# Scans that read PSUM, and a router that shares the turning banks, in a fused linear attention and mixture-of-experts kernel

## The chip, the core and the metric

The kernel runs on one core of a Trainium2 chip, in one launch. A core has five engines with a queue of instructions each: TensorE (PE in the profile), VectorE (DVE), ScalarE (ACT), GpSimd (POOL) and SyncE (SP), which here only starts transfers. They meet through semaphores. Data lie in SBUF, the on-chip memory of 128 partitions, and in PSUM, eight banks into which TensorE writes its products. The metric is the device time of one launch in microseconds; it was 355.39 as the median of 3 runs, between 354.56 and 355.56.

## The reference

Two layers follow each other. The first is a gated linear attention over 4 batches, 8 heads, 768 tokens and a head width of 48; its result is turned into 3072 tokens of 384 values. The second is a mixture of 8 experts that sends every token to the one expert with the largest logit.

```python
# attention, per batch and head
state = alpha[t][:, None] * state + outer(k[t], v[t])   # 48 x 48, alpha in 0.8 .. 1.0
y[t] = q[t] @ state
...
# mixture of experts; x is (3072, 384)
logits = x @ w_gate + modality_bias[modality_id]
e_idx = np.argmax(logits, axis=1)
probs = softmax(logits); gate_w = probs[token, e_idx]
out[mask_e] = gate_w * (np.maximum(x[mask_e] @ w1[e], 0.0) @ w2[e])   # 384 -> 1024 -> 384
```

## The kernel before

**The loop.** The attention runs in NU = 24 steps, one per chunk of 128 tokens of one batch, for all 8 heads. Heads go in pairs: 112 partitions hold two heads' channels (48 and 48, with a gap), and KW = 512 columns hold four pairs of 128 tokens. A step's turned rows (`tn`, 1600 floats on each of 112 partitions, 700 KB) hold keys, queries and the gates alpha. VectorE makes two scans over the gates. The first runs backwards (`decay`, L277): a running product of alpha, set to a top value at each chunk's last token by a constant tile DR, with max; its result GF lies in a PSUM bank, and the keys times GF are `kh`. The second runs forwards (`decay_back`, L287): it starts from the reciprocals of GF at the chunk's first token, which a tile DF holds (zero elsewhere), with add, and overwrites GF; the queries times that are `qh`. `amin` (L281) is the chunk's whole decay. TensorE then makes `scores` (L312) from qh and kh, `state` (L332), `outputs` (L339), `update` of the running 48 x 48 states (L357), and transposes: `natural` (L300) turns kh, `rows` (L370) turns the finished output. ScalarE copies PSUM results out, GpSimd masks the scores (L317) and keeps the states (L361, L363), and SyncE loads and stores.

**The router runs along.** Products for the logits (L382, L396), ranks of tokens among those of the same expert (L471 to L477), counts (L571) and places (L607) are spread over the steps as Python generators; `advance(spot)` moves each on by one piece at three spots of a step: after `rows`, after `decay_back`, and, for pieces tagged PEQ, between the scores and the outputs. Their small products lie in a PSUM bank of their own, "rt", from which VectorE reads them. Two banks "tr" turn in a ring for `natural`, `rows` and `update`. Tokens of two experts are placed early, from the tokens known by then: `route_early` counts them, `places` makes a table entry, and `gather` fetches their rows by an indirect transfer of GpSimd.

**After the loop** the first early expert runs in plain fp32 (`first_unit`, L149) while the router finishes. From then on weights and activations are split in a high and a low part of fp32r, made by ScalarE and VectorE (`split`, L876 and L878), and each product is three matmuls (L1051 to L1053 in the second layer, L1070 to L1072 in the first). `store` scales rows by gathered gates (L1085) and GpSimd scatters them. `gates_flow` makes the gates of a stretch of tokens: exponentials on ScalarE (L713), sum and reciprocal on VectorE (L714 to L716), a transpose on TensorE (L719), a copy (L721) and a store; its second use covers the last four of the first 24 groups of tokens, the four that the first use left out.

**The order** of instructions on TensorE, VectorE and ScalarE is the order in which the code issues them, in the loop and behind it; GpSimd's too in the loop. Nothing is rescheduled, so an instruction that waits holds up all behind it on its engine.

## Time and profile before

| | |
|---|---|
| median of 3 runs | 355.39 us (354.56 to 355.56) |
| profiled execution, its span | 355.34 us, 353.6 us |
| busy: PE, DVE, ACT, POOL | 337.0, 214.0, 178.8, 166.4 us |
| the loop of 24 steps | about 4 to 124 us of the span |
| transfers of turned rows | 22 of 700.0 KB, the first two chunks in parts |

The page's lists give, for a group of equal instructions, their line, engine, names and shapes, the count, the busy time and mean of one, then the idle time of the engine just before them and what ended it. A row of the list of waits gives engine, tile and line, what it waited for, and total, times, longest. A row of a timeline gives start and length in microseconds from the start of the span, and in brackets the idle time of the engine before it. A stretch is a row of windows: its busy times per engine with the number of instructions, then PEclk, the TensorE clock that was granted as a share of the full one, the share of the transfer engines that was busy, and GB/s.

### The profile page before, as it was taken

What the parts mean: (1) busy time and instruction counts of PE and PEld (TensorE: products, weight loads), DVE (VectorE), ACT (ScalarE), POOL (GpSimd) and SP (SyncE); (2) the same over time, 40 slices, a digit from 0 to 9 for tenths busy, and PEclk for the clock granted to TensorE, in tenths of its full rate; (3) what the DMA queues carried; (4) which work ended last, traced back from release to release, by engine and by line L of the source; (5) the groups of instructions that cost most, each with busy time, mean ns of one, the idle gap of its engine ahead of it and who ended that gap; (6) DMA issues with size and microseconds to landing.
All of it is one profiled execution on the core that took longest, in us unless ns stands there. A gap on an engine that the chain in (4) does not pass through costs nothing. (4 is left out here: it accounts for less than half of the span.)

```text
span 353.6 us, 8671 instructions
## 1 busy us (share of the span) xinstructions
PE 337.0 (95%) x3419; PEld 291.8 (83%) x3419; DVE 214.0 (61%) x406; ACT 178.8 (51%) x341; POOL 166.4 (47%) x210
## 2 busy tenths in 40 slices
PE   8996999999989999998999999999999999999992
PEld 3775888888768778998989988998899888888991
DVE  6899979999999658876465054605442545045400
ACT  3675587778775543474554153425432534255310
POOL 8799386658584630462673256025512661220021
PEclk9999899999998999999999999999999999999998
DMA  8999897979952957968465156316531653010011
GB/s 240 267 282 283 227 285 210 253 228 258 245 170 81 384 182 279 328 211 295 130 191 180 49 181 219 91 44 219 185 97 60 219 180 115 22 46 4 2 46 52
DMA packets 29590, 62.23 MB, mean 176 GB/s; under 512 B 3401, under 2 KB 17896, under 8 KB 29540
## 3 DMA queue, kind: packets, MB, share of 16 engines
q1 hardware_dynamic: 25396, 51.83, 49.0%
q0 software_dynamic: 4000, 9.68, 8.0%
q8 instruction: 29, 0.48, 0.6%
q14 instruction: 21, 0.17, 0.1%
q10 hardware_dynamic: 144, 0.08, 0.1%
HBM read 52.12 MB, written 9.50 MB: 174 GB/s over the span
## 5 line engine op out<-in xcount | busy, mean ns | idle before, releaser
L1017 POOL DMA_INDIRECT out_dram<-os,odx x23 | 24.7, 1073 | 101.5 <-ACT os L1085 93.7
L1051 PE MATMUL sc<-w2H,hH 128*128 128x384 f32 x192 | 65.1, 339 | 0.0
L1053 PE MATMUL sc<-w2H,hL 128*128 128x384 f32 x192 | 64.2, 334 | 0.0
L1052 PE MATMUL sc<-w2L,hH 128*128 128x384 f32 x192 | 64.2, 334 | 0.0
L878 DVE TENSOR_TENSOR w1L<-w1r,w1H 128x768 fp32r<-128x768 f32 x24 | 22.0, 956 | 65.4 <-ACT w1H L876 62.6
L317 POOL TENSOR_SCALAR_AFFINE_SELECT scT<-scT 128x512 f32<-128x512 f32 x48 | 41.7, 891 | 28.8 <-ACT scT L316 28.7
L1070 PE MATMUL tr<-xH,w1H 128*128 128x512 f32 (+1 forms) x144 | 53.8, 374 | 0.0
L1072 PE MATMUL tr<-xH,w1L 128*128 128x512 f32 (+1 forms) x144 | 53.5, 372 | 0.0
L1071 PE MATMUL tr<-xL,w1H 128*128 128x512 f32 (+1 forms) x144 | 53.5, 371 | 0.0
L870 DVE SCALAR_TENSOR_TENSOR hL<-tr,hH 128x512 fp32r<-128x512 f32 x47 | 32.3, 689 | 31.8 <-ACT hH L868 27.0
L868 ACT ACTIVATE hH<-tr 128x512 fp32r<-128x512 f32 x47 | 28.0, 598 | 44.3 <-PE tr L1072 28.1
L1085 ACT ACTIVATE os<-sc,gg 128x384 f32<-128x384 f32 x23 | 13.4, 582 | 66.8 <-PE sc L1053 40.8
L736 POOL DMA_INDIRECT gg<-gd,idx x25 | 26.9, 1078 | 27.9 <-DMA gd<-gs 20.8
L1051 PEld LDWEIGHTS sc<-w2H,hH 128*128 128x128 f32 x192 | 36.0, 188 | 1.1 <-issue 1.0
L1052 PEld LDWEIGHTS sc<-w2L,hH 128*128 128x128 f32 x192 | 36.1, 188 | 0.0
L1053 PEld LDWEIGHTS sc<-w2H,hL 128*128 128x128 f32 x192 | 36.0, 188 | 0.0
L277 DVE TENSOR_TENSOR_SCAN kv<-tn,DR 112x512 f32<-112x512 f32 x24 | 32.9, 1373 | 3.5 <-DMA tn<-in_turned_dram 2.9
L730 POOL DMA_INDIRECT xg<-xd,idx x25 | 26.5, 1058 | 12.2 <-issue 4.6
L316 ACT COPY scT<-sc 128x512 f32<-128x512 f32 x48 | 25.8, 589 | 11.9 <-PE sc L312 11.6
L1072 PEld LDWEIGHTS tr<-xH,w1L 128*128 128x128 f32 x144 | 27.1, 188 | 4.7
L1070 PEld LDWEIGHTS tr<-xH,w1H 128*128 128x128 f32 x144 | 27.1, 188 | 4.6
L1071 PEld LDWEIGHTS tr<-xL,w1H 128*128 128x128 f32 x144 | 27.1, 188 | 4.6
(247 smaller groups left out, 601.2 us busy)
## 6 DMA issues: line engine op xcount, KB each, us to landing
tn<-in_turned_dram SPq DMA_DIRECT2D x22, 700.0 KB
w1r<-in_moe_w_dram SPq DMA_DIRECT2D x16, 768.0 KB
w2r<-in_moe_w_dram SPq DMA_DIRECT2D x16, 768.0 KB
vt<-in_rowsv_dram SPq DMA_DIRECT2D x24, 192.0 KB
xd<-xs SPq DMA_DIRECT2D x24, 192.0 KB
tn<-in_turned_dram SPq DMA_DIRECT2D x4, 224.0 KB
tn<-in_turned_dram SPq DMA_DIRECT2D x2, 252.0 KB
xg<-xd,idx POOLq DMA_INDIRECT x25
```

The source lines that it names most:

```text
L277: vec.tensor_tensor_scan(GF[:, ::-1], alphas(i, 1, KW + 1)[:, ::-1], DR[:, ::-1], 0.0, op0=ALU.mult, op1=ALU.max)
L317: pool.affine_select(s, s, [[0, NP], [1, P]], ALU.is_ge, 0.0, base=0, channel_multiplier=-1)
L730: pool.indirect_dma_start(xg[x][:, u], None, xd[0:rows], IOA(idx[:, c : c + 1], 0), bounds_check=rows - 1, oob_is_err=False)
L736: pool.indirect_dma_start(gg[x][:, u : u + 1], None, gd[0:rows], IOA(idx[:, c : c + 1], 0), bounds_check=rows - 1, oob_is_err=False)
L868: act.activation(hH, hp, AF.Relu)
L870: vec.scalar_tensor_tensor(hL, hp, 0.0, hH.bitcast(F32), op0=ALU.max, op1=ALU.subtract)
L1051: pe.matmul(op, hH[:, us] if f is None else hH[:, f, us], wH, start=first, stop=False)
L1052: pe.matmul(op, hH[:, us] if f is None else hH[:, f, us], wL, start=False, stop=False)
L1053: pe.matmul(op, hL[:, us] if f is None else hL[:, f, us], wH, start=False, stop=final)
L1070: pe.matmul(hp, wH[:, d, fs], XH[:, d, :n], start=(d == 0), stop=False)
L1071: pe.matmul(hp, wH[:, d, fs], XL[:, d, :n], start=False, stop=False)
L1072: pe.matmul(hp, wL[:, d, fs], XH[:, d, :n], start=False, stop=(d == ND - 1))
```

## The change

**The scans.** DR moves to a PSUM bank (the one "rt" had); its top value is 2^-20 instead of 1. DF and the two GpSimd fills of it go. The reciprocals are taken inside GF, just before the second scan, and that scan runs in place, GF to GF, with max instead of add. `amin` is scaled back by 2^20 in one instruction. The turned rows carry 16 columns behind the second half instead of 64, 1552 floats in all.

One chunk's step on VectorE, before (DR and DF are the constant tiles, kv is the bank of GF, tn the turned rows):

```order
L277 SCALAR_TENSOR_TENSOR kv<-tn_83,DR 112x512
L280 RECIPROCAL DF_141<-kv 112x4
L281 TENSOR_TENSOR amin<-kv,tn_83 112x4
L283 TENSOR_TENSOR kh<-tn_83,kv 112x512
L287 SCALAR_TENSOR_TENSOR kv<-tn_83,DF_141 112x512
L289 TENSOR_TENSOR qh<-tn_83,kv 112x512
```

and now:

```order
L280 SCALAR_TENSOR_TENSOR kv<-tn_83,DR 112x512
L283 SCALAR_TENSOR_TENSOR amin<-kv,tn_83 112x4
L287 TENSOR_TENSOR kh<-tn_83,kv 112x512
L291 RECIPROCAL kv<-kv 112x4
L292 SCALAR_TENSOR_TENSOR kv<-tn_83,kv 112x512
L294 TENSOR_TENSOR qh<-tn_83,kv 112x512
```

The reciprocal has moved from behind the first scan to directly ahead of the second, and no instruction of the step reads two large inputs from SBUF.

**The router's products.** "rt" shares the two turning banks in the loop. A new helper `settle` has ScalarE copy such a product to an SBUF tile "kept", which VectorE reads; behind the loop it does nothing. There are nine such copies. A fourth spot END stands at the end of a step, behind `update`, and the early count takes it. On TensorE, at the step of the first early count, before (ohs are the counts so far, ones a constant):

```order
L332 MATMUL y<-qh,T_146 64x128 x8
L312 MATMUL sc<-qh,kh 64x128 x16
L571 LDWEIGHTS ones
L571 MATMUL rt<-ohs,ones 128x8
L339 MATMUL y<-scT,vt_88 64x128 x8
L357 MATMUL tr<-vt_89,knat 64x48
```

and now:

```order
L362 MATMUL tr<-vt_89,knat 64x48
L362 MATMUL tr<-vt_89,knat 48x48
L583 LDWEIGHTS ones
L583 MATMUL tr<-ohs,ones 128x8
L305 MATMUL tr<-ident,kh 128x112 x4
L375 MATMUL tr<-ident,yt 128x128 x4
```

The count has moved from between the scores and the outputs to behind the update's last product, and into a turning bank.

**Smaller moves.** Two GpSimd operations that make `hz` go ahead of the loop. `places` is split: the indices are made at once, ahead of the gather, and the positions of all early tokens once, later. At the start of the MoE the index operations stand ahead of the second split of the first-layer weights, and `gates_flow` starts one piece sooner: its exponentials right behind the four splits, its transpose L719 behind the first block of 18 first-layer products instead of the third, its store ahead of a weight load. One more store of tokens stands ahead of the first weights on SyncE. On VectorE there, before (w1L and w2L are low parts of weights, hL of activations, gt the gates):

```order
L670 TENSOR_TENSOR meta<-more,fli 1x1
L878 TENSOR_TENSOR w1L<-w1r_95,w1H 128x768 x2
L870 SCALAR_TENSOR_TENSOR hL<-tr,hH 128x512
L878 TENSOR_TENSOR w2L<-w2r_96,w2H 128x768
L714 TENSOR_REDUCE sm<-ls 128x4
L715 TENSOR_SCALAR sm<-sm 128x4
L716 RECIPROCAL gt<-sm 128x4
L870 SCALAR_TENSOR_TENSOR hL<-tr,hH 128x512
```

and now:

```order
L685 TENSOR_TENSOR meta<-more,fli 1x1
L894 TENSOR_TENSOR w1L<-w1r_95,w1H 128x768 x3
L729 TENSOR_REDUCE sm<-ls 128x4
L730 TENSOR_SCALAR sm<-sm 128x4
L731 RECIPROCAL gt<-sm 128x4
L886 SCALAR_TENSOR_TENSOR hL<-tr,hH 128x512
```

The three gate operations have moved from behind the first activations and a second-layer split to directly behind the first-layer splits.

The diff:

```diff
...
 NP = H // 2
 W = 64 + D
 KW = NP * P
-AW = KW + 64
+AW = KW + 16
 RW = 2 * KW + AW
 DM = H * D
 E = 8
...
 NJ = N // T
 MID = 2048
 EMPTY = 8192
-ALPHA_MAX_BITS = 0x3FA00000
+ALPHA_MAX_BITS = 0x3F800000
 AMIN = 1.0e-17
 AFLOOR = 1.0e-30
+TOP = 2.0**-20
 
 GROUPS = ((7, 0, 8), (15, 8, 16), (19, 16, 20), (23, 20, 24))
 LB = 4
...
     ps = ctx.enter_context(tc.tile_pool(name="ps", bufs=1, space=PSUM))
     loop_ps = ExitStack()
     lps = loop_ps.enter_context(tc.tile_pool(name="lps", bufs=1, space=PSUM))
-    ring = {"tr": (lps, "tr", 2), "rt": (lps, "rt", 1), "lg": (lps, "tr", 2)}
+    ring = {"tr": (lps, "tr", 2), "rt": (lps, "tr", 2), "lg": (lps, "tr", 2)}
 
     def ring_tile(r, shape):
         p, name, bufs = ring[r]
...
 
     def place(shape):
         return ring_tile("rt", shape)
+
+    def settle(t, shape):
+        if ring["rt"][0] is not lps:
+            return t
+        c = sb.tile(shape, F32, name="kept", bufs=2)
+        act.copy(c, t)
+        return c
 
     def turns(shape):
         return ring_tile("lg", shape)
...
-    mi = ac.tile([NU, P, 2], I32, name="mi")
-    DR = na.tile([W, KW], F32, name="DR")
+    mi = na.tile([NU, P, 2], I32, name="mi")
+    DR = lps.tile([P, KW], F32, name="DR")[:W]
     vec.memset(DR, AFLOOR)
-    vec.memset(DR[:, P - 1 :: P], 1.0)
-    DF = []
-    for i in range(2):
-        t = na.tile([W, KW], F32, name=f"DF{i}")
-        pool.memset(t, 0.0)
-        DF.append(t)
+    vec.memset(DR[:, P - 1 :: P], TOP)
     na.tile([P, 56], F32, name="padr")
     T1 = []
     for i in range(3):
...
         vec.tensor_tensor_scan(
             GF[:, ::-1], alphas(i, 1, KW + 1)[:, ::-1], DR[:, ::-1], 0.0, op0=ALU.mult, op1=ALU.max
         )
-        vec.reciprocal(DF[i % 2][:, ::P], GF[:, ::P])
-        vec.tensor_tensor(amin[:, i], GF[:, ::P], alphas(i, KW + 1, KW + 1 + NP), op=ALU.mult)
+        vec.scalar_tensor_tensor(
+            amin[:, i], GF[:, ::P], 1.0 / TOP, alphas(i, KW + 1, KW + 1 + NP), op0=ALU.mult, op1=ALU.mult
+        )
         kh = sb.tile([W, NP, P], F32, name="kh", bufs=3)
         vec.tensor_tensor(kh.rearrange("p a b -> p (a b)"), keys(i, 0), GF, op=ALU.mult)
         st[i, "k"] = kh
 
     def decay_back(i):
-        vec.tensor_tensor_scan(GF, alphas(i, 0, KW), DF[i % 2], 0.0, op0=ALU.mult, op1=ALU.add)
+        vec.reciprocal(GF[:, ::P], GF[:, ::P])
+        vec.tensor_tensor_scan(GF, alphas(i, 0, KW), GF, 0.0, op0=ALU.mult, op1=ALU.max)
         qh = sb.tile([W, NP, P], F32, name="qh", bufs=3)
         vec.tensor_tensor(qh.rearrange("p a b -> p (a b)"), keys(i, 1), GF, op=ALU.mult)
         st[i, "q"] = qh
...
         lp = turns([P, n, E]) if ring["lg"][0] is ps else place([P, n, E])
         for c in range(n):
             pe.matmul(lp[:, c], st[i, "l"][:, c], lsum, start=True, stop=True)
-        st[i, "lp"] = lp
+        st[i, "lp"] = settle(lp, [P, n, E])
 
     def logits_sum(i, n):
         z = slice(i + 1 - n, i + 1)
...
     odx = cp.tile([P, NH], I32, name="odx")
 
 
-    PEQ = "pe"
+    PEQ, END = "pe", "end"
 
     def route_begin():
         vec.memset(ohs, 0.0)
...
                 rp[:, t + 1 - t0 :], ones, oh[:, t].unsqueeze(1).broadcast_to([P, m, E]), start=False, stop=False
             )
         pe.matmul(rp, ones, ohs.unsqueeze(1).broadcast_to(sh), start=False, stop=True)
+        rp = settle(rp, [P, n, E])
         if side:
             yield
         vec.tensor_tensor(rk[:, s], rp, oh[:, s], op=ALU.mult)
...
     pos = cp.tile([P, NH], F32, name="pos")
     emp = cp.tile([P, NH], F32, name="emp")
 
+    hz = cp.tile([P, NS], F32, name="hz")
+    pool.tensor_scalar(hz, iof[:, 1 : NS + 1], float(U), None, op0=ALU.mult)
+    pool.tensor_scalar(hz, hz, zc, None, op0=ALU.is_le)
+
     def half_index():
-
-        hz = cp.tile([P, NS], F32, name="hz")
-        pool.tensor_scalar(hz, iof[:, 1 : NS + 1], float(U), None, op0=ALU.mult)
-        pool.tensor_scalar(hz, hz, zc, None, op0=ALU.is_le)
         vec.tensor_reduce(sz, hz, axis=AX.X, op=ALU.add)
 
-    def places(tp, z):
+    def places_in(tp, z):
+        vec.tensor_scalar(idx[:, z], tp, float(MID), 0.0, op0=ALU.add, op1=ALU.max)
+        vec.tensor_copy(vals[:, z], tp)
+
+    def places_out(z):
         v, p, e = vals[:, z], pos[:, z], emp[:, z]
-        vec.tensor_scalar(idx[:, z], tp, float(MID), 0.0, op0=ALU.add, op1=ALU.max)
-        vec.tensor_copy(v, tp)
         vec.tensor_scalar(p, v, 0.0, -1.0, op0=ALU.is_gt, op1=ALU.mult)
         vec.tensor_scalar(e, v, 0.0, float(EMPTY), op0=ALU.is_equal, op1=ALU.mult)
         vec.tensor_tensor(e, e, v, op=ALU.add)
-        return vec.scalar_tensor_tensor(odx[:, z], p, float(MID), e, op0=ALU.add, op1=ALU.add)
+        vec.scalar_tensor_tensor(odx[:, z], p, float(MID), e, op0=ALU.add, op1=ALU.add)
+
+    def places(tp, z):
+        places_in(tp, z)
+        places_out(z)
 
     def route_early(s, t0):
 
         n = EARLY[s]
-        yield PEQ
+        yield END
         cnt = place([P, E])
         pe.matmul(cnt, ones, ohs, start=True, stop=(s == 0))
         if s:
             pe.matmul(cnt, ones, left, start=False, stop=True)
+        cnt = settle(cnt, [P, E])
         yield
         if s:
             vec.scalar_tensor_tensor(first, cnt, float(TE), taken, op0=ALU.is_ge, op1=ALU.mult)
...
         tp = place([P, 2])
         for t in range(n):
             pe.matmul(tp, OL[:, t], OHE[:, t], start=(t == 0), stop=(t == n - 1))
-        yield
-        places(tp, slice(UE * s, UE * s + UE))
+        tp = settle(tp, [P, 2])
+        yield
+        places_in(tp, slice(UE * s, UE * s + UE))
         gather(s, early_cols(s), row(n))
         yield
         if s:
...
         vec.tensor_scalar(left, taken, -float(UE), None, op0=ALU.mult)
         if s == NA - 1:
             start_keys()
+            places_out(slice(0, UE * NA))
 
     def start_keys():
         for u in range(2):
...
     def advance(spot):
         for f in list(flows):
             tag, seen = flows[f]
-            if (tag == PEQ) != (spot == PEQ) or seen in ((now["s"], 2), (now["s"], PEQ)):
+            late = seen in ((now["s"], 2), (now["s"], PEQ), (now["s"], END))
+            if spot not in {PEQ: (PEQ,), END: (END,)}.get(tag, (1, 2)) or (late and spot != END):
                 continue
             go(f, spot)
 
...
             update(s - 1)
             if s == 1:
                 fill(2)
+        advance(END)
 
     mctx.close()
     mctx.enter_context(tc.manual_schedule(engines=manual))
...
         return None if keep else put(c, os)
 
     def layer2(h, w2, x, u, c, per, keep=False):
+        return store(layer2_sum(h, w2, u, per), x, u, c, keep)
+
+    def layer2_sum(h, w2, u, per):
         us = slice(u * P, (u + 1) * P)
         op = ps.tile([P, DM], F32, name="sc", bufs=2)
         for f in range(NF):
             j, z = divmod(f, per)
             hf = h[j] if per == 1 else (h[j][0][:, z], h[j][1][:, z])
             products(op, None, hf, piece(w2[f // 2], f % 2), us, f == 0, f == NF - 1)
-        return store(op, x, u, c, keep)
+        return op
 
     def short(x, w, c):
         xp = ps.tile([P, ND, P], F32, name="sc", bufs=2)
...
 
     prep(1, UE)
     w1s = [split1(1, 0)]
-    layer2(hs[0], w2s[0], 0, 0, 0, 2)
-    w1s += [split1(1, 1)]
+    op0 = layer2_sum(hs[0], w2s[0], 0, 2)
     for _ in ends:
         pass
     gather(2, slot_cols(1))
+    store(op0, 0, 0, 0)
+    w1s += [split1(1, 1)]
     layer2(hs[0], w2s[0], 0, 1, 1, 2)
     w1s += [split1(1, j) for j in (2, 3)]
     seq = [("E", 1)] + [("S", i) for i in range(1, SU - 1)] + [("H", SU)] + [("S", SU - 1)]
     cols = [early_cols(0)] + [early_cols(e) if k == "E" else slot_cols(e)[: 1 if k == "H" else U] for k, e in seq]
     seq = [("E", 0)] + seq
     last_gates = gates_flow(EARLY[-1], NU)
+    next(last_gates)
     weights(0, expert(seq[2][1]))
     for n in range(1, len(seq)):
         kind, e = seq[n]
```

## The prediction

> **What bounds the kernel now.** I read the page's busy shares first, then the waits of PE, then PE, VectorE and ScalarE in order of time at the two places where the change moves work.
>
> ```profile
> PE 337.0 (95%) x3419; PEld 291.8 (83%) x3419; DVE 214.0 (61%) x406; ACT 178.8 (51%) x341; POOL 166.4 (47%) x210
> PE sc L312 <- issue: 1.5, 1, 1.5
> PE rt L571 <- DVE ohs L490: 1.5, 1, 1.5
> PE y L332 <- issue: 1.5, 1, 1.5
> PE tr L370 <- ACT yt L347: 1.1, 5, 0.3
> PE kv L1024 <- DMA xg<-xd,idx: 0.8, 1, 0.8
> PE tr L370 <- DVE emp L562: 0.5, 1, 0.5
> PE kv L719 <- PE tr L1072: 0.3, 1, 0.3
> ```
>
> PE is busy for 337.0 of the 353.6 us of the span, and everything else is at 61% or less. So a VectorE saving is worth nothing by itself; only PE's pauses and its clock can be shortened, and a new pause is paid in full. The waits list nearly all pauses after the first 20 us: 1.5 us at L571 (the router's count), 0.5 at L370, 0.8 at L1024, 0.3 at L719, and two of 1.5 us whose cause is "issue".
>
> The pauses cost more than their length. These windows are 3.41 us long and hold, in this order, two around the pause at L332, which a window's boundary cuts, two around that at L312 and two around that at L571, and last a long one of the loop for comparison; the columns are span, busy us and instruction count per engine, then PEclk.
>
> ```profile
> 23.90:27.32 3.42, 3.06 (x53) 2.44 (x49) 3.26 (x3) 3.21 (x7) 3.36 (x4) 1.00 1.05 306
> 27.32:30.74 3.42, 2.33 (x59) 2.15 (x60) 3.25 (x6) 1.31 (x4) 3.18 (x5) 1.00 1.03 286
> 34.15:37.56 3.41, 1.89 (x30) 1.55 (x24) 2.97 (x8) 1.38 (x4) 1.45 (x3) 1.00 1.04 272
> 37.56:40.98 3.42, 3.42 (x30) 2.67 (x30) 3.32 (x7) 1.35 (x3) 1.64 (x2) 0.50 0.93 261
> 102.42:105.83 3.41, 1.94 (x56) 1.70 (x57) 3.31 (x9) 2.29 (x6) 3.10 (x4) 1.00 0.23 78
> 105.83:109.24 3.41, 3.41 (x37) 3.32 (x34) 3.31 (x6) 1.15 (x3) 1.68 (x2) 0.50 0.00 0
> 70.00:100.00 30.00, 29.57 (x593) 24.40 (x592) 28.83 (x48) 23.72 (x54) 20.17 (x23) 1.00 0.87 242
> ```
>
> A window with 1.5 us idle (3.41 - 1.89, 3.41 - 1.94) is followed by one at a granted clock of 0.50; a window with 1.1 idle (3.42 - 2.33) is not. A stretch at 0.50 does half of 3.41 us of work: about 1.7 us lost. So the pause at L571 costs 1.5 + 1.7 = 3.2 us. The Trainium skill (TensorE: Matmul & The Clock Gate, What's actually happening) says the same of the windows, 3413 ns at half rate or full, and adds that they are free-running; by that, which pause falls whole into one window changes between executions. No trace here shows a second execution.
>
> **Part 1, the scans.** One step of VectorE, with the wait at its end:
>
> ```profile
> 43.72 1.68 DVE L277 TENSOR_TENSOR_SCAN kv<-tn,DR 112x512 f32<-112x512 f32 x1
> 45.43 0.18 DVE L280 RECIPROCAL DF<-kv 112x4 f32<-112x4 f32 x1
> 45.53 0.13 DVE L281 TENSOR_TENSOR amin<-kv,tn 112x4 f32<-112x4 f32 x1
> 45.58 0.68 DVE L283 TENSOR_TENSOR kh<-tn,kv 112x512 f32<-112x512 f32 x1
> 46.29 1.23 DVE L287 TENSOR_TENSOR_SCAN kv<-tn,DF 112x512 f32<-112x512 f32 x1
> 47.56 0.69 DVE L289 TENSOR_TENSOR qh<-tn,kv 112x512 f32<-112x512 f32 x1
> 50.51 0.17 DVE L555 TENSOR_REDUCE sz<-hz 128x1 f32<-128x13 f32 x1 [2.26 <-POOL hz L554]
> 50.59 1.23 DVE L277 TENSOR_TENSOR_SCAN kv<-tn,DR 112x512 f32<-112x512 f32 x1
> L277 DVE TENSOR_TENSOR_SCAN kv<-tn,DR 112x512 f32<-112x512 f32 x24 | 32.9, 1373 | 3.5 <-DMA tn<-in_turned_dram 2.9
> L287 DVE TENSOR_TENSOR_SCAN kv<-tn,DF 112x512 f32<-112x512 f32 x24 | 30.1, 1255 | 0.6
> L283 DVE TENSOR_TENSOR kh<-tn,kv 112x512 f32<-112x512 f32 x24 | 16.2, 676 | 0.0
> L317 POOL TENSOR_SCALAR_AFFINE_SELECT scT<-scT 128x512 f32<-128x512 f32 x48 | 41.7, 891 | 28.8 <-ACT scT L316 28.7
> ```
>
> The same scan takes 1.23 or 1.68 us. The products L283, which already take their second input from PSUM, keep to 0.68 throughout. I take it that a scan with two SBUF inputs is held up by GpSimd's work and one with its second input in PSUM is not. Then 48 scans at 1.23 are 59.0 instead of 63.0 us: -4.0. Against it: the reciprocal now hides, since L281 starts 0.10 after it; in its new place the scan waits for its result, so it costs about 0.2 instead of 0.1, and 24 of these are +2.4. The two index operations of POOL go ahead of the loop: the wait of 2.26 at L555 goes. VectorE gains 4.0 - 2.4 + 2.3 = 3.9 us by the loop's end.
>
> The Trainium skill (SBUF — State Buffer, Who interferes with whom) states this rule: two SBUF inputs contend with a GpSimd read, one does not. The rows of L277 and L283 agree.
>
> PE takes almost none of that: from 70 to 100 us it is busy for 29.57 of 30.00, and no pause in the list but the named ones is over 0.3 us. It may start its full stretch earlier, since in the first steps it does follow VectorE. A step's excess of scans is 4.0 / 24 = 0.17 us against 0.10 for the reciprocal, so four or five steps give 0.3, and the turned rows, 3% smaller (1552 floats for 1600), land a little sooner where VectorE waits for them (2.9 us in all at L277). I take -0.4, between 0 and -0.8.
>
> No row shows a scan with its second input in PSUM, nor one in place there. Bounds: 1.23, and 1.73 (the slowest scan now is of that order). I take 1.23, as products with and without PSUM do not differ that way; the rival below has the other end. The max in place of add is the same pass.
>
> **Part 2, the shared banks and the count.** Nine small ScalarE copies come in; the nearest row is the state's copy, 0.32 for 112x192, so about 0.2 each, 2 us of an engine at 51%. The copies of the logits stand behind score copies for which PE's next group does not wait. The count is different, and it is the main term:
>
> ```profile
> 102.88 1.05 PE L312 MATMUL sc<-qh,kh 48*64 48x128 f32 x32
> 105.40 0.17 PE L571 MATMUL rt<-ohs,ones 128*128 128x8 bf16 x1 [1.47 <-DVE ohs L490]
> 105.50 1.70 PE L339 MATMUL y<-scT,vt 128*64 128x128 f32 x16
> 104.95 0.40 DVE L490 TENSOR_TENSOR ohs<-ohs,hsum 128x8 bf16<-128x8 bf16 x1
> 101.43 0.32 ACT L359 COPY S<-tr 112x192 f32<-112x192 f32 x1
> ```
>
> Now it stands ahead of the outputs and makes PE wait until 105.35. Moved behind the update, it comes after the outputs' products, of which the row shows 1.70 us at half clock, so some 0.9 at full, and the update's, about half as much: 103.9 + 1.4 = 105.3, and VectorE, ahead by then, has its input earlier than 105.35. The wait is gone: -1.5, and the half-clock stretch behind it: -1.7. New: the count takes a turning bank right after the update's, so the next transposes (L300) wait for the copy of S: 0.3 + 0.1 = +0.4. The wait of 0.5 at L370 for the last of the place operations shrinks, since those move to later: -0.3. VectorE's lead does not run out: it gains 3.9 and PE 3.5.
>
> Loop: -1.5 - 1.7 + 0.4 - 0.3 - 0.4 = **-3.5**.
>
> **Part 3, the start of the MoE.** The last early gates' transpose (L719) moves on PE from behind the third block of first-layer products to behind the first. Blocks are 18 matmuls, 2.16 us. What it needs comes in this order (before's times):
>
> ```profile
> 151.61 0.28 PE L1070 MATMUL tr<-xH,w1H 128*128 128x256 f32 x1
> 153.76 0.28 PE L1070 MATMUL tr<-xH,w1H 128*128 128x256 f32 x1
> 158.56 0.27 PE L719 MATMUL kv<-ident,gt 128*4 128x128 f32 x1 [0.32 <-PE tr L1072]
> 153.10 0.58 ACT L1085 ACTIVATE os<-sc,gg 128x384 f32<-128x384 f32 x1 [0.83 <-DMA gg<-gd,idx]
> 153.58 1.56 ACT L876 CAST w1H<-w1r 128x768 fp32r<-128x768 f32 x2
> 154.70 1.83 DVE L878 TENSOR_TENSOR w1L<-w1r,w1H 128x768 fp32r<-128x768 f32 x2
> 157.91 0.18 DVE L714 TENSOR_REDUCE sm<-ls 128x4 f32<-128x32 f32 x1
> 158.33 0.18 DVE L716 RECIPROCAL gt<-sm 128x4 f32<-128x4 f32 x1
> ```
>
> In the new order PE would issue it at 153.8. The exponentials stand on ScalarE behind both casts (end 155.1), and these behind a store that waits for the gathered gates until 153.1. VectorE takes the sum behind the two low parts; these can begin when the first cast is done, about 154.4, and end at 156.2; sum to reciprocal is 0.6 more: 156.8. So PE waits 3.0. If the gates' gather were no limit, the store could go at about 151.8, as its products end when the first-layer ones begin (151.61), and all of it 1.3 earlier: 1.7. I take 2.7, nearer the measured end. In exchange the old waits go: 0.3 at L719, and 0.8 at L1024, whose gathers have that much longer. A pause of 2.7 puts more than 1.5 into one window nearly wherever the boundary falls: +1.7 for a half-clock stretch. Behind it all work is as before. Start of MoE: 2.7 - 0.3 - 0.8 + 1.7 = **+3.3**.
>
> The other moves (index operations before a split, a store of tokens ahead of the first weights, one ahead of a weight load) are off this path: none of them issues anything that PE's two changed pauses wait for.
>
> **Sum.** 353.6 - 3.5 + 3.3 = 353.4 of span, and with the 1.7 outside it (355.34 - 353.6) 355.1; the median of the runs, 355.39, is 0.05 above the profiled one. Forecast **355.2 us**, no change that can be measured: a difference under 0.3% (1.07 us) counts as none, since the runs of before spread over 1.0 us. Its own range is 354.3 to 356.4.
>
> **Rivals.** (a) The gate transpose's wait is short or cut by a window's boundary and costs no clock, so the gain of the loop shows: 355.2 - 1.7 = 353.5. For it: the gather that sets it lands late behind weight loads and could land sooner. Against: 1.5 in one window was enough twice. Chance 0.20.
>
> (b) The stretch at 37.56 goes too. Its pause starts at 34.34, just inside the window from 34.15; begun 0.4 earlier it leaves 1.3 in that window, between the 1.1 that did nothing and the 1.5 that did. 353.5, or with (a) 351.8. Chance 0.17, and 0.07 for both.
>
> (c) Slower: the gate transpose waits the full 3.0 and the boundary halves it, so that both windows hold 1.5 idle. Then the clock stays at half through the tail of the second and the whole third: 1.9/2 + 1.7 = 2.6 instead of 1.7, and with 0.3 more of wait and no gain in the first steps (0.4) 356.8. It decides from a wait of about 2.9 on. Chance 0.14.
>
> (d) Slower by the scans: at 1.37 each (L277's mean now) they take 48 x 0.14 = 6.7 us more than I assume. VectorE's gain becomes a loss of 2.8; PE then waits for it in the later steps, the loop's gain of 3.5 is lost and some clock with it: 359. It decides from about 0.08 us per scan. Against: products reading PSUM are not slower. Chance 0.06.
>
> The rest, 0.36, is the forecast.
>
> **How the numbers follow.** Faster: (a), (b) and both, 0.44. Slower: (c), (d) and a little of the forecast's upper edge, 0.22. Same: 0.34. The range from 351.5 to 357.2 takes in both (a) with (b) and (c) and leaves out (d) and the far ends.
>
> **What would show it.** Right: no wait at the count's matmul; scans all near 1.23; a wait of PE of 2 to 3 us for the reciprocal of the gates ahead of the second block of first-layer products; a clock of 0.50 behind it, none near 100 us. Wrong: no pause at the gate transpose (then 352 to 353.5), or scans over 1.3.

## The result

The changed kernel took 359.62 us as the median of 17 executions (355.92 to 362.46); the kernel before, beside it, 354.06 us (352.36 to 356.68). The ratio is 1.0119, with a 95% interval from 1.0089 to 1.0149: it is slower, by about 1.2%. A second series of ten executions gave 357.47 beside 354.46, a ratio of 1.0070 (1.0036 to 1.0103): slower again, by less. A ratio leaves out the executions more than 1.5% above the fastest of their kernel, while a median takes all, so that a kernel can have a ratio near 1 and a median 2 us above. The profiled execution of the changed kernel took 357.0 us with a span of 355.2, so it is one of its better ones. That matters below: the mean granted clock of an execution ran from 0.966 to 0.989, with a mean of 0.977, where the kernel before has 0.990 over the 138 executions that stood beside the experiments.

The waits of PE in the changed kernel, longest first, answer to the list of before:

```profile
PE kv L734 <- DVE gt L731: 2.6, 1, 2.6
PE tr L620 <- DVE OHE L614: 2.3, 1, 2.3
PE sc L317 <- issue: 1.0, 1, 1.0
PE y L337 <- issue: 0.9, 1, 0.9
PE tr L583 <- DVE ohs L496: 0.7, 1, 0.7
PE tr L375 <- ACT S L364: 0.5, 1, 0.5
```

Two waits are new. One is the gates' transpose (L734, was L719), 2.6 us, where 2.7 had been forecast. The other is the early places' product (L620, was L607), 2.3 us; nothing of that was forecast. The wait at the count (L583) has halved and not gone. The two pauses for which nothing shown is to blame are shorter, 0.9 and 1.0 instead of 1.5, and the half-clock stretch that began at 37.56 before is gone. Each of the new waits leaves PE idle for over 2 us of one window of 3.41 us (3.41 - 1.10, 3.41 - 1.38), and a window at half clock follows (columns as before):

```profile
112.72:116.13 3.41, 1.10 (x34) 0.85 (x25) 3.24 (x11) 1.23 (x3) 1.22 (x2) 1.00 1.03 386
116.13:119.55 3.42, 2.94 (x34) 2.77 (x31) 2.38 (x8) 0.91 (x2) 0.72 (x1) 0.50 1.05 380
153.68:157.09 3.41, 1.38 (x12) 1.38 (x13) 3.34 (x7) 1.92 (x5) 2.52 (x3) 1.00 0.90 268
157.09:160.51 3.42, 3.42 (x18) 3.42 (x17) 0.98 (x3) 1.32 (x2) 1.91 (x2) 0.50 1.02 392
```

VectorE's groups of one step and GpSimd's masks, now, and the last product of the queries on VectorE, now (L294) and before (L289):

```profile
L292 DVE TENSOR_TENSOR_SCAN kv<-tn,kv 112x512 f32<-112x512 f32 x24 | 29.5, 1228 | 0.8
L280 DVE TENSOR_TENSOR_SCAN kv<-tn,DR 112x512 f32<-112x512 f32 x24 | 29.4, 1226 | 3.1 <-DMA tn<-in_turned_dram 2.4
L283 DVE SCALAR_TENSOR_TENSOR amin<-kv,tn 112x4 f32<-112x4 f32 x24 | 3.9, 161 | 0.8
L322 POOL TENSOR_SCALAR_AFFINE_SELECT scT<-scT 128x512 f32<-128x512 f32 x48 | 29.9, 646 | 52.4 <-ACT scT L321 52.2
...
117.22 0.69 DVE L294 TENSOR_TENSOR qh<-tn,kv 112x512 f32<-112x512 f32 x1
```

```profile
117.94 0.69 DVE L289 TENSOR_TENSOR qh<-tn,kv 112x512 f32<-112x512 f32 x1
```

Both scans are at 1.23 us, as forecast, and GpSimd's masks have fallen from 891 to 646 ns: the scans and GpSimd no longer hold each other up. But VectorE reaches its last product of the queries only 0.7 us sooner (117.94 - 117.22), not 3.9.

### The profile page after: what moved, and what is told of

Same layout as the page of the kernel before. It is cut to its first block, busy times and chain, and to the rows that moved or that the text cites. A ratio compares the mean times of both kernels' runs of the same rounds, so it can differ in the third digit from the quotient of the medians.

```text
span 355.2 us, 8689 instructions
## 1 busy us (share of the span) xinstructions
PE 336.4 (95%) x3419; PEld 291.5 (82%) x3419; DVE 214.5 (60%) x402; ACT 179.9 (51%) x350; POOL 135.8 (38%) x208
## 5 line engine op out<-in xcount | busy, mean ns | idle before, releaser
L1034 POOL DMA_INDIRECT out_dram<-os,odx x23 | 23.0, 1002 | 111.3 <-ACT os L1102 98.6
L1089 PE MATMUL tr<-xH,w1L 128*128 128x512 f32 (+1 forms) x144 | 54.3, 377 | 0.0
L322 POOL TENSOR_SCALAR_AFFINE_SELECT scT<-scT 128x512 f32<-128x512 f32 x48 | 29.9, 646 | 52.4 <-ACT scT L321 52.2
L1089 PEld LDWEIGHTS tr<-xH,w1L 128*128 128x128 f32 x144 | 27.9, 194 | 4.7
L1087 PEld LDWEIGHTS tr<-xH,w1H 128*128 128x128 f32 x144 | 27.9, 194 | 4.6
L280 DVE TENSOR_TENSOR_SCAN kv<-tn,DR 112x512 f32<-112x512 f32 x24 | 29.4, 1226 | 3.1 <-DMA tn<-in_turned_dram 2.4
```

The source lines that it names most:

```text
L280: vec.tensor_tensor_scan(GF[:, ::-1], alphas(i, 1, KW + 1)[:, ::-1], DR[:, ::-1], 0.0, op0=ALU.mult, op1=ALU.max)
L322: pool.affine_select(s, s, [[0, NP], [1, P]], ALU.is_ge, 0.0, base=0, channel_multiplier=-1)
L1087: pe.matmul(hp, wH[:, d, fs], XH[:, d, :n], start=(d == 0), stop=False)
L1089: pe.matmul(hp, wL[:, d, fs], XH[:, d, :n], start=False, stop=(d == ND - 1))
```

## The experiments

Sixteen kernels were run, one of them the changed kernel again. Times are medians; "beside" is the kernel before, run beside it; the ratio has its 95% interval. The clock is the mean over the executions, without single ones of over 370 us.

| run | time | beside | ratio | clock |
|---|---|---|---|---|
| changed kernel | 359.62 | 354.06 | 1.0119 (1.0089 to 1.0149) | 0.977 |
| gates back | 359.8 | 354.94 | 1.0100 (1.0044 to 1.0157) | 0.982 |
| count back | 357.86 | 354.94 | 1.0055 (1.0017 to 1.0093) | 0.983 |
| both back | 357.54 | 354.94 | 1.0007 (0.9963 to 1.0050) | 0.987 |
| places at the end | 361.3 | 354.94 | 1.0135 (1.0071 to 1.0199) | 0.978 |
| loop only | 355.9 | 354.51 | 1.0030 (0.9990 to 1.0070) | 0.987 |
| MoE start only | 357.21 | 354.51 | 1.0079 (1.0050 to 1.0109) | 0.984 |
| count only | 355.25 | 354.51 | 1.0027 (0.9995 to 1.0059) | 0.987 |
| second scan only | 354.85 | 354.51 | 1.0012 (0.9981 to 1.0043) | 0.991 |
| index operations only | 353.34 | 354.46 | 0.9972 (0.9942 to 1.0002) | 0.993 |
| index operations and count | 354.68 | 354.46 | 1.0000 (0.9971 to 1.0029) | 0.992 |
| changed kernel again | 357.47 | 354.46 | 1.0070 (1.0036 to 1.0103) | 0.980 |
| idle matmuls, too long | 356.82 | 354.46 | 1.0086 (1.0056 to 1.0116) | 0.993 |
| idle matmuls, sized | 356.27 | 354.83 | 1.0022 (0.9988 to 1.0056) | 0.991 |
| index operations and smaller rows | 355.38 | 354.83 | 1.0009 (0.9975 to 1.0043) | 0.988 |
| index operations, again | 353.19 | 354.15 | 0.9980 (0.9945 to 1.0015) | 0.992 |
| the same with idle matmuls | 353.68 | 354.15 | 0.9976 (0.9938 to 1.0015) | 0.994 |

Medians of 6 or 12 executions are not exact to a microsecond: "both back" lies 2.6 us above its neighbour by the medians and has a ratio of 1.0007. Where two medians differ and the intervals of the ratios overlap, the difference is not shown.

### Undoing parts of the change

**Gates back.** The gates' flow starts one piece later again.

```diff
     last_gates = gates_flow(EARLY[-1], NU)
-    next(last_gates)
```

> The changed kernel, with only the last early gates started where they were before: exponentials behind the first block of first-layer products, transpose on PE behind the third. Theory A (the time comes from two new waits of PE, 2.6 us for the gates' reciprocal and 2.3 us for the places' one-hots, and the half clock behind each, 1.7 us): the wait of 2.6 and its half-clock stretch go, old waits of about 0.3 and 0.8 us return, so 3 us less than the changed kernel's 359.6: 356.5. Theory B (the loop itself is slower, by copies and small VectorE work): within 1 us of 359.6.

359.8 in six executions, no gain that can be seen. The wait of 2.6 us at the transpose is gone (0.4 is left), and another has come in its place; the first rows of the list of waits:

```profile
PE tr L620 <- DVE OHE L614: 2.3, 1, 2.3
PE sc L317 <- issue: 2.1, 1, 2.1
PE kv L1041 <- DMA xg<-xd,idx: 1.7, 2, 1.5
```

PE now waits 1.7 us for the gathered tokens of the next expert, and a stretch at half clock follows, from 169.11. In the changed kernel the wait at the transpose had covered this. That is why theory A's number was missed, as far as one profile can say it.

**Count back.** The early count stands between scores and outputs again.

```diff
         n = EARLY[s]
-        yield END
+        yield PEQ
```

> The changed kernel, with only the early count back between the scores and the outputs. Theory A: PE waits about 1.5 us at the count again, and the wait of 2.3 us for the places' one-hots shrinks by as much, since PE comes to them later: one wait of the two remains with a half-clock stretch, so 359.6 within 1 us. The prediction's own theory (the count's place is worth 3.2 us): 362.8.

357.86, 1.8 below the first series of the changed kernel and 0.4 above the second; the ratios overlap. The wait at the count is 2.2 us, and the one for the places is not in the list any more. So the count's new place did not save 3.2 us, which would have made this run 362.8. Whether it cost anything is not shown by this run.

**Both back.**

> The changed kernel, with both the gates and the count back in their old places; left are the scans in PSUM, the shared banks with their copies, the smaller rows and the earlier index work. Theory A: as with the gates alone, 356.5 within 1 us, so 2 above the kernel before. If scans and copies by themselves gain (the prediction): under 354.

357.54, 1 us over what theory A had, at a ratio that shows no loss. Its profiled execution came to the first early expert 2.1 us sooner than the kernel before (at 123.76 instead of 125.88) and lost that at the gathers:

```profile
PE kv L1041 <- DMA xg<-xd,idx: 4.4, 2, 2.2
```

**Places at the end.** The gates back, and the places' products behind the update as well.

```diff
-        yield PEQ
+        yield END
         tp = place([P, 2])
```

> The changed kernel with the gates back and, new, the early places' products also at the end of a step, behind the update, where the count stands. Theory A: the wait for the one-hots falls from 2.3 to about 0.8 us and its half-clock stretch goes, beside what the gates give: 359.6 - 3 - 1.5 - 1.7 = 353.4, about the kernel before. Theory B: 358 or more.

361.3, the slowest. The wait for the one-hots fell from 2.3 to 1.3 us, as far as the new place gave, and the next PE instruction that needs VectorE waited 1.8 instead. Here are the waits for VectorE in the order of the program, count, places, ranks:

```profile
PE tr L583 <- DVE ohs L496: 0.7, 1, 0.7
PE tr L620 <- DVE OHE L614: 1.3, 1, 1.3
PE sc L476 <- DVE oh L473: 1.8, 1, 1.8
```

Their sum is 3.8 us, against 0.7 + 2.3 = 3.0 in the changed kernel. So PE's wait does not hang on the place of one product: near the loop's end VectorE is behind, and moving a product that needs it changes where PE waits.

### Parts by themselves

**Loop only.** The changed kernel with count, gates and the start of the MoE as before; left are the scans, the shared banks and copies, the smaller rows and the earlier index work. The part of the edit at the start of the MoE (the other two are shown above):

```diff
-    op0 = layer2_sum(hs[0], w2s[0], 0, 2)
+    layer2(hs[0], w2s[0], 0, 0, 0, 2)
+    w1s += [split1(1, 1)]
     for _ in ends:
         pass
     gather(2, slot_cols(1))
-    store(op0, 0, 0, 0)
-    w1s += [split1(1, 1)]
```

> The changed kernel with the count back, the gates back and the start of the MoE in its old order (store and second split ahead of the index operations); left are the scans in PSUM, the shared banks with their copies, the smaller rows and the index work ahead of the loop. Theory C (with the count and the gates back, the time is lost at the start of the MoE, where the next expert's weights now start about 1.3 us sooner and crowd the gathers that PE waits for): like the kernel before, 354 to 355, some 2.5 us under the run with both back. Theory D (scans, copies or the VectorE work of the router cost it): 357 or more, as that run.

355.9, 1.4 above the kernel beside it, which its interval does not tell from nothing. By the medians it is 1.6 under the run with both back, as theory C has it, but the ratios, 1.0030 and 1.0007, show no such difference; only the profiles speak for theory C. The wait for the gathers is 0.5 us here and 4.4 there. The two issues of the next expert's first weights, among which the gathers are issued, take 2.44 us from the first start to the second end in the run with both back and 3.65 here:

```profile
152.50 2.44 SPq L717 DMA_DIRECT2D w1r<-in_moe_w_dram  x2
```

```profile
153.39 3.65 SPq L717 DMA_DIRECT2D w1r<-in_moe_w_dram  x2
```

So with the index operations ahead of the second split, the second load starts sooner, and the gathers land later: PE's last wait for them ends at 164.35 there and at 162.31 here. This rests on one profile of each; that the crowding is the cause was not tested by itself. Among the profiles with the old order this wait varies too, from 0.4 to 1.8 us, so only 4.4 and the 4.1 of the run with the places at the end stand clear of it.

**MoE start only.** The kernel before with the new order there, gates included (the reverse of the two edits above).

> The kernel before, with only the new order at the start of the MoE: index operations and gather ahead of store and second split, gates started one piece sooner. By the prediction's third part: 2.7 - 0.3 - 0.8 of waits and 1.7 of half clock, 354.9 + 3.3 = 358.2. Theory C and D alike expect a loss here, C 2 to 3 us; if the gates' wait only takes the place of a wait for the gathers, within 1 us of before.

357.21, 2.7 above the kernel beside it, clear of noise; the forecast's third part had 3.3. PE waits where it was forecast:

```profile
PE kv L719 <- DVE gt L716: 2.9, 1, 2.9
```

**Count only.** The kernel before with the spot END and the count there (the two main lines of the edit).

```diff
-        yield PEQ
+        yield END
...
+        advance(END)
```

> The kernel before, with only the early count moved to the end of a step, behind the update. By the prediction: the wait of 1.5 us and its half-clock stretch go, 354.9 - 3.2 = 351.7. Theory A (the wait moves on to the places' one-hots, since VectorE and not the place sets the time): 354.9 within 1 us, with PE waiting 1 to 2 us at the places' products. Slower than 356: the count's place delays the chain of count, places and gathers.

355.25, 0.7 above the kernel beside it, and within its interval of no change; theory A. The wait of 1.5 us has come apart, again into waits for VectorE and ScalarE, and the gathers are waited for longer (1.8 us instead of 0.8):

```profile
PE kv L1026 <- DMA xg<-xd,idx: 1.8, 2, 1.7
PE tr L300 <- DVE kh L283: 1.4, 1, 1.4
PE tr L370 <- DVE vals L560: 1.1, 1, 1.1
PE rt L396 <- ACT scT L316: 0.7, 1, 0.7
PE rt L571 <- DVE ohs L490: 0.6, 1, 0.6
```

**Second scan only.** Reciprocals inside GF, in place, with max; DR stays in SBUF.

```diff
-        vec.reciprocal(DF[i % 2][:, ::P], GF[:, ::P])
-        vec.tensor_tensor(amin[:, i], GF[:, ::P], alphas(i, KW + 1, KW + 1 + NP), op=ALU.mult)
+        vec.scalar_tensor_tensor(
+            amin[:, i], GF[:, ::P], 1.0 / TOP, alphas(i, KW + 1, KW + 1 + NP), op0=ALU.mult, op1=ALU.mult
+        )
...
-        vec.tensor_tensor_scan(GF, alphas(i, 0, KW), DF[i % 2], 0.0, op0=ALU.mult, op1=ALU.add)
+        vec.reciprocal(GF[:, ::P], GF[:, ::P])
+        vec.tensor_tensor_scan(GF, alphas(i, 0, KW), GF, 0.0, op0=ALU.mult, op1=ALU.max)
```

> The kernel before, with only the second scan changed: reciprocals inside GF just ahead of it, in place with max, no DF; the first scan keeps DR in SBUF. Second scans near 1.23 us instead of 1.255 (0.6 us in all), reciprocals no longer hidden (+2.4) and amin in the two-step form (+1.6): VectorE 3 us later at the loop's end. Theory D: since PE waits for VectorE at the count and later, 1 to 3 us slower than before, 356 to 358. If PE's lag behind VectorE covers it: 354.9 within 1 us.

354.85, no change that can be told. It shows the scans best, for one form stands beside the other: second inputs in SBUF for the first scan, in PSUM for the second. GpSimd's masks fall to 657 ns with it alone, so most of their gain comes from the second scan.

```profile
L273 DVE TENSOR_TENSOR_SCAN kv<-tn,DR 112x512 f32<-112x512 f32 x24 | 31.0, 1292 | 4.0 <-DMA tn<-in_turned_dram 3.4
L285 DVE TENSOR_TENSOR_SCAN kv<-tn,kv 112x512 f32<-112x512 f32 x24 | 29.5, 1228 | 0.8
```

**Index operations only.** Two small operations of GpSimd leave the loop.

```diff
+    hz = cp.tile([P, NS], F32, name="hz")
+    pool.tensor_scalar(hz, iof[:, 1 : NS + 1], float(U), None, op0=ALU.mult)
+    pool.tensor_scalar(hz, hz, zc, None, op0=ALU.is_le)
+
     def half_index():
-
-        hz = cp.tile([P, NS], F32, name="hz")
-        pool.tensor_scalar(hz, iof[:, 1 : NS + 1], float(U), None, op0=ALU.mult)
-        pool.tensor_scalar(hz, hz, zc, None, op0=ALU.is_le)
         vec.tensor_reduce(sz, hz, axis=AX.X, op=ALU.add)
```

> The kernel before, with only the two index operations of GpSimd moved ahead of the loop, so that VectorE no longer waits 2.3 us for them at step 9. If VectorE's lead decides at the count (theory A): its input comes 2.3 us sooner than 105.35, the wait of 1.5 us at the count and its half-clock stretch go: 354.6 - 3.2 = 351.4. If PE or the clock takes it back elsewhere: 354.6 within 1 us.

353.34, 1.1 under the kernel beside it. The same again:

> The kernel before with the two index operations ahead of the loop, once more. If the gain is real: 353.3 to 353.9, about 1 us under the kernel before, mean clock about 0.993. If it was chance: within 0.5 us of before.

353.19, 1.0 under. Each interval just takes in no change; the two agree, and the clock is up from 0.990 to 0.992 or 0.993. The forecast of 3.2 was too much: PE still waits 1.5 us at the count (2.1 in the second run), since it came there as much sooner as VectorE did: 101.58 instead of 103.93, and VectorE's input at 103.00 instead of 105.35.

**Index operations and count.** Both of the last edits on the kernel before.

> The kernel before, with the two index operations ahead of the loop and the count at the end of the step. Theory A: VectorE's 2.3 us are there for the places too, so neither the count nor the places make PE wait: 351.4, as with the index operations alone. If the count's place is bad in itself (a bank that waits for the copy of the states, later gathers): 0.5 to 1 us more than that.

354.68, as the kernel before, and 1.3 above the run without the count's move. No wait at the count, and 2.1 us at the places in its stead:

```profile
PE rt L607 <- DVE L L401: 2.1, 1, 2.1
```

**Index operations and smaller rows** (`AW = KW + 16`).

> The kernel before, with the index operations ahead of the loop and the smaller turned rows (1552 floats for 1600). If fewer bytes help in the first 40 us, where the transfers are busy throughout and PE waits for its instructions: 0.3 to 1 us under the run with the index operations alone (353.3). If not: the same within 0.5 us.

355.38, and a ratio of 1.0009: the smaller rows give nothing that can be seen here. The 1 us of the index operations does not show in this run either.

### The half clock by itself

**The changed kernel again.**

> The changed kernel once more, for a second profile and more times. If the slow executions differ from the profiled one by the granted clock alone: mean clock near 0.977 again, time near 359.3, and a profile with waits of PE at the same places but more or longer stretches at 0.50 than the two of the first profile. If by something else: other waits of 2 us or more.

357.47, clock 0.980. The same waits, 2.8 and 2.3 us, and again two stretches of one window each in the profiled execution, which at 355.92 us is again one of the better ones. The longer executions have on the whole the lower clock: over the first 17, 0.0233 of 359.1 us went with the half clock on average, 8.4 us, over those of the kernel before 0.0101 of 354.6, 3.6. The difference, 4.8, is as large as that of the mean times; but some of it lies inside the waits and costs nothing there, so it bounds the loss and does not measure it.

A profile of a long execution at a low clock came with the run that has the gates back (361.6 us, clock 0.972). It has three stretches. The first two, each with the window before it:

```profile
32.58:35.99 3.41, 1.74 (x52) 1.18 (x42) 3.24 (x5) 1.31 (x4) 0.62 (x2) 1.00 1.06 255
35.99:39.41 3.42, 3.02 (x22) 2.67 (x23) 0.77 (x3) 1.26 (x3) 1.22 (x2) 0.50 1.04 274
39.41:42.82 3.41, 3.41 (x29) 2.66 (x29) 3.24 (x5) 1.29 (x3) 0.00 (x0) 0.50 0.75 180
117.91:121.33 3.42, 1.84 (x48) 1.82 (x48) 3.25 (x10) 0.82 (x3) 1.22 (x2) 1.00 1.05 398
121.33:124.74 3.41, 2.93 (x36) 1.86 (x34) 2.06 (x12) 1.51 (x4) 1.38 (x2) 0.50 1.02 362
124.74:128.15 3.41, 3.41 (x56) 3.08 (x52) 0.00 (x0) 0.97 (x3) 2.21 (x4) 0.50 0.58 177
```

These two are two windows long; the third, from 169.11, is one. In each of the two the first window at half clock itself has 0.4 or 0.5 us idle (3.42 - 3.02, 3.41 - 2.93), the end of the wait or the one behind it, and the clock stays down for another: 3.4 us of loss for a wait, not 1.7. That is no rule: the window from 116.13 in the changed kernel has as much idle (3.42 - 2.94), and full clock follows it.

**Idle matmuls in the waits.** PE is kept busy while it waits; the products are overwritten.

```diff
         yield END
-        cnt = place([P, E])
+        cnt = place([P, KW])
+        if s == 0:
+            for _ in range(4):
+                pe.matmul(cnt, still[:, :P], still, start=True, stop=True)
+        cnt = cnt[:, :E]
...
+            for _ in range(10):
+                pe.matmul(tp, still[:, :P], still, start=True, stop=True)
...
+            for z4 in range(20):
+                pe.matmul(gp[:, :P], ident, ident, start=True, stop=True)
```

> The changed kernel with idle matmuls put ahead of the three PE instructions that wait: 4 of 512 columns (0.24 us each) ahead of the early count, 10 ahead of the early places, 20 of 128 columns in fp32 (0.11 us each) ahead of the last gates' transpose; their products are overwritten. The waits stay as long as they are, but PE is busy in them. If it is the half clock behind the waits that makes the kernel slow: the stretches behind these places go, mean clock up from 0.977 to about 0.985, 359.3 - 3 to 4.5 = 355 to 356. If it is the waits alone: no change, 359.3 within 1 us, or slower by what the idle matmuls add.

356.82, clock 0.993: no stretch at half clock is left behind the three places (one is left, from 38.19, behind a pause of the first 40 us). But the 20 matmuls in fp32 last 4.6 us, 2 more than the wait. So the run was repeated with the waits' own lengths (3, 9 and 10 matmuls):

> The changed kernel with idle matmuls of the waits' own length: 3 of 512 columns ahead of the early count, 9 ahead of the early places (the 9 that ran took 2.3 us, the wait), 10 in fp32 of 128 columns ahead of the last gates' transpose (20 took 4.6 us, the wait is 2.6). If the half clock is all of the loss: mean clock 0.99, and 359.1 - 4.7 = 354.4, within 1 us of the kernel before. If a second cause is left: 356 or more at that clock.

356.27, clock 0.991. The matmuls fill the waits (the trace lacks one record of each of the first two groups, and shows two records for a matmul in fp32):

```profile
106.51 0.82 PE L585 MATMUL tr<-still 128*128 128x512 bf16 x2
116.31 2.12 PE L625 MATMUL tr<-still 128*128 128x512 bf16 x8
156.32 2.39 PE L744 MATMUL kv<-ident 128*128 128x128 f32 x20
```

With every wait kept, the mean time is 356.8 us, against 358.7 over all 27 executions of the changed kernel: the half clock behind these waits is a cause by itself, worth about 2 us (2.0 between the two means, 0.3 to 3.6 by their spread) of the 4.2 between 358.7 and the 354.5 beside. It is not all; the forecast of this run, 354.4 within 1 us, is missed. What is left, some 2 us, is of the size of the waits themselves, less those that they replaced (2.6 + 2.3 + 0.7 against 1.5 + 0.5 + 0.8 + 0.3). Part of it may be chance: in the profile of this run the pauses of the first 40 us for which nothing shown is to blame add up to 4.0 us (1.4, 1.8 and 0.8), in the changed kernel's first to 2.6. The idle matmuls need not be the cause, since the profile with the gates back, which has none, has 4.3 (1.2, 2.1 and 1.1).

**The same in the kernel with the index operations moved**, 5 idle matmuls ahead of its count.

> The same with 5 idle matmuls of 512 columns (1.2 us) in the wait of 1.5 us at the early count. If that wait still costs half clock in some executions: mean clock 0.995 and 0.5 to 1 us under the run without them. If not: the same time, or up to 0.3 us more.

353.68, clock 0.994: no further gain.

## Why the prediction was wrong, point by point

- **The scans (right).** Both at 1.23 us, in place and from PSUM; rival (d) is out.
- **VectorE gains 3.9 us (wrong, the step that failed first).** It gained 0.7 in the first profile of the changed kernel and 1.7 in the second. To see where the rest went, take for each instruction of VectorE, up to the last product of the queries, by how much it ends later than all before it, and add the idle time ahead of it; these sums are compared with the kernel before. The terms that the forecast had are nearly as forecast: both scans -3.5 (forecast -4.0), reciprocals together with `amin` +2.5 (forecast +2.4, put on the reciprocals alone; `amin` now stands where nothing hides it, and the reciprocals cost less), the wait for the index operations -2.35 (forecast -2.3). These rows show the pair and the product behind the second scan, in the kernel before and in the changed one (the row of `amin` now stands above):

```profile
L280 DVE RECIPROCAL DF<-kv 112x4 f32<-112x4 f32 x24 | 4.4, 185 | 1.0
L281 DVE TENSOR_TENSOR amin<-kv,tn 112x4 f32<-112x4 f32 x24 | 3.1, 130 | 0.0
L289 DVE TENSOR_TENSOR qh<-tn,kv 112x512 f32<-112x512 f32 x24 | 16.5, 687 | 1.6
```

```profile
L291 DVE RECIPROCAL kv<-kv 112x4 f32<-112x4 f32 x24 | 4.5, 188 | 0.6
L294 DVE TENSOR_TENSOR qh<-tn,kv 112x512 f32<-112x512 f32 x24 | 16.5, 687 | 2.3 <-PE tr L305 0.5
```

  Put at nothing were two: 0.65 us more of idle time ahead of the product of the queries, in both profiles, and the router's work on VectorE, 1.8 us more in the first profile and 0.9 in the second. Of that, the sum of the logits, which now reads two inputs from SBUF, is +0.7 in the first and -0.2 in the second. Before, the five took 0.18 or 0.19 us each. Their row now in the first profile (least, middle and greatest in ns), and one of them beside GpSimd's masks:

```profile
L406 DVE TENSOR_TENSOR L<-kept,bt x5: 183/184/655, 36.5 to 115.1; 128x32 f32<-128x32 f32 x5
...
54.21 0.66 DVE L406 TENSOR_TENSOR L<-kept,bt 128x32 f32<-128x32 f32 x1
53.60 1.22 POOL L322 TENSOR_SCALAR_AFFINE_SELECT scT<-scT 128x512 f32<-128x512 f32 x2 [2.72 <-ACT scT L321]
```

  The one at 54.21 ends with GpSimd's masks, 53.60 + 1.22. By the rule that the prediction named (the Trainium skill, SBUF — State Buffer, Who interferes with whom) this follows: `kept` and the bias are two SBUF inputs where a PSUM bank was one of them. The rule was applied to the scans alone. The other +1.1, in both profiles, is not shown to come from the change: these 37 small operations took 8.6 us in the profile of the kernel before and 9.7 in the changed kernel's two, but 8.6 to 10.1 in the eight other profiles of kernels where the router still reads PSUM.
- **"VectorE's lead does not run out" (wrong).** At the count, the places and the ranks PE waits for VectorE, 3.0 us in the changed kernel and 3.8 when the places move too. PE's own gain is part of it. At the early places PE was ready at 117.11 before and at 112.95 now (111.85 + 1.10), 4.2 us sooner, and VectorE's one-hots at 116.21 and 115.21, 1.0 sooner. The rows, before and then now:

```profile
116.02 0.19 DVE L601 TENSOR_TENSOR OHE<-OHE,tok 128x32 f16<-128x32 f16 x1
117.11 0.55 PE L607 MATMUL rt<-OHE,OL 128*128 128x2 f16 x16
```

```profile
111.85 1.10 PE L317 MATMUL sc<-qh,kh 48*64 48x128 f32 x32
115.02 0.19 DVE L614 TENSOR_TENSOR OHE<-OHE,tok 128x32 f16<-128x32 f16 x1
115.27 0.55 PE L620 MATMUL tr<-OHE,OL 128*128 128x2 f16 x16 [2.31 <-DVE OHE L614]
```

  Had VectorE been 3.9 sooner, PE would not have waited there (112.3 against 112.95). Some of PE's lead may be luck of the execution: in the first profile its pauses in the first 40 us were 1.1 us shorter and no half clock followed them, as rival (b) had it. The count's place, forecast at -3.2, saved nothing in any run. In the three pairs that differ in it alone and ran side by side the late place is slower by 0.7 (count only against before), 1.3 (with the index operations) and 2.3 us (with the gates back), none of them clear of noise by the ratios' intervals.
- **The gates' transpose (right).** 2.6 us of wait where 2.7 was forecast, a half-clock stretch behind it, no wait for the gathers left; +2.7 us for that part by itself where 3.3 was forecast. What was not seen is that undoing the gates alone gives nothing, since a wait for the gathers returns (1.7 to 4.4 us, where the forecast had taken out 0.8) behind the new order of the index operations. That the wait came out within 0.1 us is in part luck: 2.7 was chosen between 1.7 and 3.0, and the second profile has 2.8, the run with the count back 2.3.
- **One half-clock stretch of 1.7 us per wait (mis-sized).** Two windows in a row occur: 5 of the 29 stretches in the 18 profiles (without the one behind each execution's last product), all 5 in kernels with the gates back. The two profiles of the changed kernel, with two single stretches each, stand at the good end: by the clock, up to 4.8 us more go with it on average than in the kernel before, and idle matmuls get back about 2. Where the longer executions have their other stretches no profile shows.
- **The sum.** Forecast: loop -3.5, start of the MoE +3.3. Measured apart: loop without the count +1.4, count +0.7, start of the MoE +2.7, together 4.8; the whole is 5.6 in medians in the first series and 3.0 in the second. Of the parts only the start of the MoE is clear of noise by itself. Rival (c), slower by a longer half clock, comes nearest, at another place and size.

## What to carry to other kernels

Where one engine is nearly saturated and a second only just keeps ahead of it, a wait that is moved can come back at the next instruction that needs the second engine; count the second engine's work in full, small operations included, before calling a wait gone. Price a pause of the matrix engine at its length plus up to two half-clock windows, and compare mean clocks over many executions, since one profile can show the lucky case. Moving a small operand from PSUM to SBUF can put its readers in the way of another engine, in some executions more than in others (the five sums took 1.9 and 1.1 us here, 0.9 before).

## What was not expected of the hardware

- The windows' phase differs between executions. Half-clock stretches begin at 37.56 in the kernel before, 116.13 in the changed one, and 35.99 with the gates back; after whole windows of 3.413 us are taken away, 0.0, 0.1 and 1.9 us are left. So the same pause falls whole into a window in one execution and is cut in the next. The prediction named this from the Trainium skill (TensorE: Matmul & The Clock Gate, What's actually happening); the runs agree.
- The idle time that brings the clock down is no fixed number. These two windows, of the run with the count back and of the one with both back, had 0.74 us idle (3.41 - 2.67) and 1.60 (3.42 - 1.82), each the end of a pause that a boundary cuts (1.5 and 2.2 us in all); the first was followed by half clock, the second was not:

```profile
34.71:38.12 3.41, 2.67 (x35) 2.30 (x35) 2.81 (x6) 1.32 (x4) 1.22 (x2) 1.00 1.01 291
38.12:41.54 3.42, 3.42 (x44) 2.78 (x46) 3.25 (x5) 2.15 (x5) 0.00 (x0) 0.50 0.64 190
```

```profile
101.71:105.13 3.42, 1.82 (x35) 1.75 (x36) 3.21 (x8) 1.33 (x5) 1.34 (x2) 1.00 0.02 4
105.13:108.54 3.41, 3.39 (x72) 2.29 (x70) 3.20 (x12) 2.56 (x7) 1.10 (x2) 1.00 0.02 5
```

  So the prediction's bounds, nothing at 1.1 and half clock at 1.5, held in the one profile that it had and not beyond. What else enters was not tested.
